# A fused attention and soft-MoE kernel on one core: routing logits in column groups, and a new order of the work inside a step

## The chip, the core and the metric

The kernel runs on one NeuronCore of a Trainium2 chip. The metric is the device time of one launch in microseconds (us); lower is better. A time is stated as the median of the runs taken, and beside it stands one profiled execution, from which every duration below is read. TensorE does matrix products and transposes, ScalarE does exponentials and copies, VectorE does copies, reciprocals and additions, GpSimd (POOL) masks and issues some loads, and the SyncE queue (SP) issues the other loads and all stores.

## The reference

The program is an attention over 8 batches of 8 heads, followed by a soft mixture of experts on the result:

```python
# q, k, v: (8, 8, 576, 64); beacon_k, beacon_v: (8, 8, 16, 64)
k_all, v_all = concat(beacon_k, k), concat(beacon_v, v)     # 592 keys per head
s = q @ k_all.T / 8;  causal mask on the 576, none on the 16 beacons
x = softmax(s) @ v_all                                      # -> (4608, 512)

logits = x @ phi                                            # (4608, 32): 8 experts x 4 slots
d = exp(logits); d /= d.sum(0)                              # over the 4608 tokens, per slot
slot_input = d.T @ x                                        # (32, 512)
slot_out[e] = relu(slot_input[e] @ w1[e]) @ w2[e]           # 512 -> 1024 -> 512
c = exp(logits); c /= c.sum(1)                              # over the 32 slots, per token
out = c @ slot_out                                          # (4608, 512)
```

So one array of exponentials, exp(x @ phi), serves twice: summed over tokens per slot, and over slots per token. (The reference subtracts maxima and adds a tiny constant to the sums, which changes nothing that matters for the time.)

## The kernel before

**Attention loop.** The loop over n runs over 32 pairs of heads; batch b is n // 4 and g is n % 4. Queries and keys are held as 16 beacon positions plus 576 tokens, 592 columns, cut in 5 chunks of 128 (the last has 80). For a pair, `transp(n, 0)` and `transp(n, 1)` turn q and k by 18 small TensorE transposes each (L265) into a PSUM tile `tr`, and VectorE copies them out (L271; ScalarE does it for a few early pairs). `score(n, st)` with st = 0 to 3 makes the transposed scores of four groups of key chunks (L282) into two PSUM tiles `sc`, used in turn: steps 0 and 2 use the first, steps 1 and 3 the second, so step 2 has to wait for the exponential of step 0, and the next pair's step 1 for that of step 3. ScalarE takes the exponential (L289), and GpSimd then zeroes the upper triangle of the diagonal blocks (L291). `attend_head(n, a)` multiplies the 15 blocks of head a with the values (L304) into one half of the PSUM tile `av`, and begins with block (0, 0), which the exponential and the mask of score step 3 make. `normalize(n)` on VectorE divides by the row sums (L314, L315) into `xb`. There is one `av`, so the next `attend_head(., 0)` follows the last `normalize`.

**Routing.** `xt_piece` turns the normalized rows (L330) into `xT`, with tokens along the free dimension. `logit_piece(b, hf)` multiplies half a batch (288 tokens) by `phih`, in which the 32 columns of phi stand four times beside each other, so that all 128 output rows carry the 32 slots four times (L344). Its exponential goes to `eLh` (L348), one long row of tokens, with the token sum taken along. `dt_piece` turns 32 rows of `eLh` back by TensorE (L356), VectorE copies the result to `dT`; `si_products` multiplies it with `xb` (L382), and `add_si` adds the product to `siacc` (L388). `col_sums` makes the sums over slots, four columns per call of a batch (L416). All PSUM tiles named `tr` share two buffers.

**The order of work** is written out by hand[...]. The first six pairs have an order of their own (`head`), and from n = 6 on each step runs the list of operations in the loop (here `s` is a score step, `T` a turn of q or k of the pair n + 2, `a` a head of the pair n - 1, `V` a turn of the values on VectorE, `C` the column sums):

```python
for op in ("s0", "s1", "Tq", "Tk", "s2", "V", "C", "a0", "dt", "s3", "lg", "xt", "lL", "si", "a1"):
    step(op, n, b, g)
```

**Loads.** q and k come on SP's queue into a ring of five pairs (L95), which `load_more` refills right after `Tk`; v comes on GpSimd's queue (L127 and neighbours), and so do the expert weights, 32 pieces of 1 MB of float32 in memory and half that on the chip (L183), at the end of a step. The last weight pieces are issued at the end of the last step.

**Tail.** After the loop come the last pair's attention, its turns, the logits of the last batch (L588, `last_logits`), the folding of `siacc` (L397), some matmuls whose result is not used (`warm_tail`, L605), the last `dt_piece`, the slot inputs (L370, L616), and the two expert layers in four passes (L642, L656), the second of which adds into `sop`. Then 9 column groups of 512 tokens are made: four matmuls of 128 tokens each (L687), copied out and scaled by ScalarE and VectorE in turn (L689, L691), and stored by SP, 1 MB per group (L695, L697).

## Time and profile before

| | |
|---|---|
| median of 5 runs | 195.86 us (195.09 to 196.31) |
| the profiled execution's own time | 195.86 us |
| its span (first to last instruction) | 193.8 us |
| TensorE busy | 157.1 us (81% of the span) |
| VectorE busy | 135.7 us (70%) |
| ScalarE busy | 129.9 us (67%) |
| GpSimd busy | 111.1 us (57%) |
| read from memory / written | 62.65 MB / 9.44 MB |
| mean granted clock of TensorE | 0.929 of full |

The profile is one execution; times in it count from the start of the span. The launch's time is 2.06 us more than its span. "Busy" is time in which an engine executes, "idle before" names what ended the wait ahead of an instruction. The matmuls' ends are modelled, and neighbouring instructions of an engine overlap a little, so the distance from one start to the next is shorter than the durations say. The DMA share is the mean busy share of the 16 DMA engines, and can exceed one where packets overlap.

### The profile page before, as it was taken

What the parts mean: (1) busy time and instruction counts of PE and PEld (TensorE: products, weight loads), DVE (VectorE), ACT (ScalarE), POOL (GpSimd) and SP (SyncE); (2) the same over time, 40 slices, a digit from 0 to 9 for tenths busy, and PEclk for the clock granted to TensorE, in tenths of its full rate; (3) what the DMA queues carried; (4) which work ended last, traced back from release to release, by engine and by line L of the source; (5) the groups of instructions that cost most, each with busy time, mean ns of one, the idle gap of its engine ahead of it and who ended that gap; (6) DMA issues with size and microseconds to landing.
All of it is one profiled execution on the core that took longest, in us unless ns stands there. A gap on an engine that the chain in (4) does not pass through costs nothing.

```text
span 193.8 us, 7205 instructions
## 1 busy us (share of the span) xinstructions
PE 157.1 (81%) x3061; PEld 108.2 (56%) x3061; DVE 135.7 (70%) x283; ACT 129.9 (67%) x190; POOL 111.1 (57%) x285
## 2 busy tenths in 40 slices
PE   6669786989887999997999797999988999787000
PEld 2437556767665777765776575577655754332000
DVE  4465587789877899996799689489845552799000
ACT  2796744789867989986788687499978222598000
POOL 8689596688776597878658567368746200000000
PEclk9975979999999999998799999699999999999955
DMA  5999999999999999999999999999999990199995
GB/s 195 266 270 350 244 283 276 264 267 271 289 260 277 297 301 270 274 252 294 267 282 283 259 308 254 238 198 205 196 213 211 215 194 14 57 405 426 411 429 225
DMA packets 20464, 50.84 MB, mean 262 GB/s; under 512 B 5456, under 2 KB 5456, under 8 KB 19408
## 3 DMA queue, kind: packets, MB, share of 16 engines
q0 software_dynamic: 8048, 21.74, 56.9%
q1 hardware_dynamic: 12240, 28.35, 39.5%
q8 instruction: 24, 0.39, 0.8%
q10 hardware_dynamic: 144, 0.29, 0.5%
q14 instruction: 8, 0.07, 0.1%
HBM read 62.65 MB, written 9.44 MB: 372 GB/s over the span
## 4 chain that ended last, share of the span: by engine, by line
PE 45%; DMA 20%; ACT 8%; DVE 7%; issue 5%; POOL 5%; SPq 1%; DVEq 0%; ACTq 0%; POOLq 0%
DMA arena<-in_k_dram 13%; PE av L304 13%; PE sc L282 10%; DMA vbuf<-in_v_dram 7%; ACT ex L289 7%; PE tr L330 4%; PE tr L265 4%; PE tr L344 3%; DVE arena L691 3%; POOL ex L291 2%; PE av L656 2%; PE sc L642 2%; DVE xb L315 2%; PE tr L382 2%; PE fp L687 1%
## 5 line engine op out<-in xcount | busy, mean ns | idle before, releaser
L289 ACT ACTIVATE ex<-sc 128x736 f16<-128x736 f32 (+1 forms) x124 | 101.5, 871 | 29.3 <-PE sc L282 26.4
L291 POOL TENSOR_SCALAR_AFFINE_SELECT ex<-ex 128x256 f16<-128x256 f16 (+1 forms) x155 | 57.8, 399 | 34.8 <-ACT ex L289 34.6
L282 PE MATMUL sc<-qT,kT 64*128 64x336 bf16 (+5 forms) x384 | 42.9, 295 | 9.0 <-ACT ex L289 4.0
L304 PEld LDWEIGHTS <-ex 128*128 128x128 f16 (+1 forms) x930 | 36.9, 108 | 11.8 <-issue 11.2
L304 PE MATMUL av<-vh,ex 128*128 128x65 f16 x840 | 39.1, 200 | 2.9 <-DVE xb L315 1.8
L265 PE MATMUL tr<-idb,arena 64*64 64x64 bf16 x1152 | 27.7, 198 | 5.0 <-DMA arena<-in_k_dram 2.9
L265 PEld LDWEIGHTS <-arena 64*64 64x64 bf16 x1152 | 23.0, 112 | 13.0 <-issue 7.0
L271 DVE COPY qT<-tr 128x576 bf16<-128x576 bf16 x32 | 23.9, 748 | 4.9 <-PE tr L265 4.7
L315 DVE TENSOR_TENSOR xb<-av,r 128x640 f16<-128x640 f32 x31 | 25.6, 824 | 1.1
L282 PEld LDWEIGHTS <-kT 64*128 64x128 bf16 (+1 forms) x384 | 16.2, 100 | 15.6 <-issue 5.8
L338 DVE COPY xT<-tr 128x592 f16<-128x592 f16 x31 | 14.0, 458 | 14.3 <-PE tr L330 14.2
L271 DVE COPY kT<-tr 128x576 bf16<-128x576 bf16 x27 | 20.3, 750 | 2.8 <-PE tr L265 2.8
L151 DVE STREAM_TRANSPOSE vh<-vbuf 128x256 f32<-128x256 f32 x32 | 20.4, 658 | 2.3 <-DMA vbuf<-in_v_dram 2.3
L183 POOL DMA_DIRECT2D arena<-in_moe_w_dram x32 | 17.9, 560 | 0.2
L127 POOL DMA_DIRECT2D vbuf<-in_v_dram x27 | 15.1, 571 | 0.2 <-issue 0.2
L330 PE MATMUL tr<-idh,xb 128*128 128x128 f16 (+1 forms) x160 | 14.4, 227 | 0.2 <-DVE xb L315 0.2
L689 ACT ACTIVATE arena<-fp,rc 128x512 f32<-128x512 f32 (+1 forms) x18 | 11.4, 676 | 4.7 <-PE fp L687 4.0
L330 PEld LDWEIGHTS <-xb 128*128 128x128 f16 (+1 forms) x160 | 10.9, 104 | 4.4 <-issue 3.4
L691 DVE TENSOR_SCALAR arena<-fp,rc 128x512 f32<-128x512 f32 (+1 forms) x19 | 12.5, 730 | 0.4 <-PE fp L687 0.4
L687 PE MATMUL fp<-soh,eLh 128*128 128x512 f16 (+1 forms) x37 | 10.8, 371 | 2.2 <-ACT arena L689 1.5
L344 PE MATMUL tr<-xT,phih 128*128 128x288 f16 x56 | 9.9, 299 | 0.2 <-DVE xT L338 0.2
L314 DVE RECIPROCAL r<-av 128x10 f32<-128x10 f32 x31 | 6.8, 220 | 4.4 <-PE av L304 3.7
(99 smaller groups left out, 134.8 us busy)
## 6 DMA issues: line engine op xcount, KB each, us to landing
arena<-in_moe_w_dram POOLq DMA_DIRECT2D x32, 512.0 KB, 9.3
arena<-in_q_dram SPq DMA_DIRECT2D x32, 288.0 KB, 15.6
arena<-in_k_dram SPq DMA_DIRECT2D x31, 288.0 KB, 15.2
out_dram<-arena SPq DMA_DIRECT2D x8, 1024.0 KB, 9.5
vbuf<-in_v_dram POOLq DMA_DIRECT2D x30, 128.0 KB, 7.7
arena<-in_v_dram POOLq DMA_DIRECT2D x4, 128.0 KB, 6.7
out_dram<-arena SPq DMA_DIRECT2D x2, 256.0 KB, 3.0
out_dram<-arena SPq DMA_DIRECT2D x1, 512.0 KB, 3.2
```

The source lines that it names most:

```text
L151: nc.vector.transpose(out=dst[:, e], in_=src.bitcast(FP).rearrange("p (j e) -> p e j", j=TK)[:, e])
L183: nc.gpsimd.dma_start(out=arena[:, wloc[m]:wloc[m] + WP], in_=src)
L265: nc.tensor.transpose(tp[po:po + 64, j, :], hi, idb[po:po + 64, po:po + 64])
L271: nc.vector.tensor_copy(out=dst, in_=src)
L282: nc.tensor.matmul(sc[0:kn, a, col:col + un], kT[n % 3][64 * a:64 * a + 64, P * c:P * c + kn], qT[n % 3][64 * a:64 * a + 64, u0:u0 + un], ...
L289: nc.scalar.activation(e, sc[:, :, 0:w], AF.Exp, scale=scale)
L291: nc.gpsimd.affine_select(out=e[0:m, :, o:o + m], in_=e[0:m, :, o:o + m], compare_op=AL.is_ge, fill=0.0, base=0, pattern=[[0, 2], [1, m]], ...
L304: nc.tensor.matmul(dst[0:m, i * DD:(i + 1) * DD], ex[n][0:kn, o + a * w:o + a * w + m], vchunk(b, 2 * g + a, c, kn), start=(c == 0), stop= ...
L315: nc.vector.tensor_tensor(out=xb[b % 2][:, :, 2 * g:2 * g + 2, :].rearrange("p i a d -> p a i d"), in0=avv[:, :, :, 0:D], in1=r5[:, :, :]. ...
L330: nc.tensor.transpose(tp[:, i, 0:m], xb[b % 2][0:m, i, 2 * g:2 * g + 2, :].rearrange("p h d -> p (h d)"), idh[0:m, 0:m])
L344: nc.tensor.matmul(lp[:, 0:w], phih[:, t, :, :].rearrange("p g s -> p (g s)"), xT[b][:, t, Nb + hf * w:Nb + (hf + 1) * w], start=(t == 0), ...
L691: nc.vector.tensor_scalar(out=osb[:, j, c], in0=fp_[:, c], scalar1=rc[:, i:i + 1], scalar2=None, op0=AL.mult)
```

## The change

The change has four parts.

1. **Column groups.** The 32 columns of phi stand in `phih` once. A batch's logits are made by 16 matmuls instead of 8: for each of the four parts of the model dimension, four matmuls whose results go to partitions 0, 32, 64 and 96, and which take every fourth block of 32 tokens, 160 columns each. The exponential of a batch is one ScalarE instruction of 128 x 160 into a compact array `eLz` at the end of `eLh`. `dt_piece` becomes one VectorE 32x32 transpose of it and a memset.
2. **Spreading.** Because the output needs the slots along 128 rows for all tokens, `spread_rows` (four matmuls with a selection matrix `rept`, and a copy of 496 columns) and `spread_ends` (three matmuls and a copy for the last 80 tokens of several batches) make `eLh` out of `eLz`. Two of these run in the tail, the others between the column groups of the output. The column sums and their reciprocals move there too, one group ahead of their use. Sums over tokens are one reduction over `eLz` and a matmul (`slot_factors`).
3. **Order in a step.** `Tq` goes between s0 and s1, the first head and `xt` go between s1 and s2, `Tk` between s2 and s3; the logits, the second head, `dt` and `si` close the step. The logits of a batch are made in the next batch's step g = 2, `dt` there too, and `si` in g = 3. In `head`, at n = 3, `turn_v(1, 1)` moves from before the attention to the end of the step.
4. **Tail.** `warm_tail` is gone; the logits of the first three parts are followed by both folds, then by the last pair's turn and the last part.

```diff
@@ -220,14 +220,19 @@
-    eLh = const.tile([P, Nb + N + P - UL], F16, name="eLh")
-    nc.vector.memset(eLh[:, Nb + N:], 0.0)
-    nc.vector.memset(eLh[:, 0:Nb], 0.0)
-    dsum9 = const.tile([P, 2 * B - 1], FP, name="dsum9")
+    ZW = NCH * 32
+    zo = N + 64 - B * ZW
+    eLh = const.tile([P, N + 64], F16, name="eLh")
+    eLz = eLh[:, zo:zo + B * ZW].rearrange("p (b i q) -> p b i q", b=B, q=32)
+    xTs = [const.tile([P, NDC * U + 48], F16, name=f"xT{i}") for i in range(2)]
+        nc.vector.memset(xTs[i][:, NDC * U:], 0.0)
+    rept = const.tile([P, 4, 4, NSL], F16, name="rept")
-    phih = const.tile([P, NDC, 4, NSL], F16, name="phih")
+    phih = const.tile([P, NDC, NSL], F16, name="phih")
...
@@ -333,34 +335,60 @@
                 idh[0:m, 0:m])
         src = tp[:, :, :].rearrange("p i u -> p (i u)")[:, 0:U]
         if act:
-            nc.scalar.activation(xT[b][:, g, :], src, AF.Copy)
+            nc.scalar.activation(xTs[b % 2][:, g * U:(g + 1) * U], src, AF.Copy)
         else:
-            nc.vector.tensor_copy(out=xT[b][:, g, :], in_=src)
-
...
+            nc.vector.tensor_copy(out=xTs[b % 2][:, g * U:(g + 1) * U], in_=src)
+
+    def logits(b, lp, ts):
+        x = xTs[b % 2][:, :]
+        for t in ts:
+            for z in range(4):
+                nc.tensor.matmul(
+                    lp[32 * z:32 * z + NSL, :], phih[:, t, :],
+                    bass.AP(tensor=x.tensor, offset=x.offset + t * U + 32 * z,
+                            ap=[x.ap[0], [P, NCH], [1, 32]]),
+                    start=(t == 0), stop=(t == NDC - 1), tile_position=(0, 32 * z))
+
+    def logit_exp(b, lp):
+        nc.scalar.activation(eLz[:, b].rearrange("p i q -> p (i q)"), lp, AF.Exp)
+
+    def logit_piece(b):
+        lp = ps_tr.tile([P, ZW], FP, name="tr", tag="tr")
+        logits(b, lp[:, :], range(NDC))
+        logit_exp(b, lp[:, :])
 
     def dt_piece(b):
         dT[b] = sml.tile([P, NCH, NSL], F16, name="dT", tag="dT", bufs=2)
-        tp = ps_tr.tile([P, NCH, NSL], F16, name="tr", tag="tr")
-        for i in range(NCH):
-            m = P if i < 4 or b == B - 1 else UL
-            nc.tensor.transpose(tp[0:m, i, :], eLh[0:NSL, b * S + P * i:b * S + P * i + m],
-                                idh[0:NSL, 0:NSL])
-        if b == B - 1:
-            nc.vector.tensor_copy(out=dT[b][:, :, :], in_=tp[:, :, :])
+        nc.vector.transpose(out=dT[b][:, :, :].rearrange("p i s -> p (i s)"),
+                            in_=eLz[:, b].rearrange("p i q -> p (i q)"))
+        nc.vector.memset(dT[b][0:Nb, 0, :], 0.0)
+
+    def spread(dst, z, src):
+        nc.tensor.matmul(dst, rept[:, z, :, :].rearrange("p t s -> p (t s)"), src,
+                         start=True, stop=True)
+
+    def evac(eng, out, in_):
+        if eng is nc.scalar:
+            nc.scalar.activation(out, in_, AF.Copy)
         else:
-            nc.vector.tensor_copy(out=dT[b][:, 0:4, :], in_=tp[:, 0:4, :])
-            nc.vector.tensor_copy(out=dT[b][0:UL, 4, :], in_=tp[0:UL, 4, :])
-        nc.vector.memset(dT[b][0:Nb, 0, :], 0.0)
+            eng.tensor_copy(out=out, in_=in_)
+
+    def spread_rows(b, eng):
+        sp = ps_tr.tile([P, 4, 4, 32], FP, name="tr", tag="tr")
+        for z in range(4):
+            spread(sp[:, :, z, :], z, eLz[:, b, 0:4, :])
+        evac(eng, eLh[:, b * S:b * S + 4 * P - Nb],
+             sp[:, :, :, :].rearrange("p i z q -> p (i z q)")[:, Nb:])
+
+    def spread_ends(b0, b1, eng, sp=None):
+        nb = b1 - b0
+        if sp is None:
+            sp = ps_tr.tile([P, nb * UL], FP, name="tr", tag="tr")[:, :]
+        spv = sp.rearrange("p (b q) -> p b q", q=UL)
+        for z in range(3):
+            w = min(32, UL - 32 * z)
+            spread(spv[:, :, 32 * z:32 * z + w], z, eLz[:, b0:b1, 4, 0:w])
+        evac(eng, eLh[:, b0 * S:b1 * S].rearrange("p (b s) -> p b s", s=S)[:, :, S - UL:], spv)
 
     def si_half(b, hf):
         sp = ps_tr.tile([P, 2, NSL], FP, name="tr", tag="tr")
...
@@ -404,17 +432,19 @@
 
     G = 4
     NG = N // (P * G)
-    csp = av[:, 0, 400:512]
+    csp = av[:, 1, 456:456 + NG * G]
     rc = const.tile([P, NG * G], FP, name="rc")
 
     def etok(cg, j):
-        o = Nb + cg * P * G
+        o = cg * P * G
         return eLh[:, o:o + P * G].rearrange("p (t j) -> p t j", j=G)[:, :, j]
 
     def col_sums(c0, c1):
+        c = slice(c0 * G, c1 * G)
         for i in range(c0 * G, c1 * G):
             nc.tensor.matmul(csp[:, i:i + 1], etok(i // G, i % G)[0:NSL], ones[0:NSL, :],
                              start=True, stop=True)
+        nc.vector.reciprocal(out=rc[:, c], in_=csp[:, c])
 
     def head(n):
         score(n, 0)
...
@@ -422,7 +452,7 @@
         score(n, 1)
         if n < 5:
             transp(m, 0)
-        for x, y in {1: ((0, 0), (0, 1)), 3: ((1, 1),), 4: ((1, 0), (1, 2))}.get(n, ()):
+        for x, y in {1: ((0, 0), (0, 1)), 4: ((1, 0), (1, 2))}.get(n, ()):
             turn_v(x, y)
         if 3 <= n < 5:
             attend_head(n - 2, 0)
@@ -461,6 +491,8 @@
                 attend_head(x, 0)
             attend_head(x, 1)
             normalize(x)
+        if n == 3:
+            turn_v(1, 1)
         if n == 4:
             turn_v(1, 3)
             transp(6, 0)
...
                     turn_v(x, y)
             if 13 <= n < 17:
                 turn_tail(1, n - 13)
-        elif op == "C" and g == 2 and b > 1:
-            col_sums(b - 2, b - 1)
         elif op[0] == "a":
             attend_head(n - 1, int(op[1]))
             if op == "a1":
                 normalize(n - 1)
         elif op == "xt":
             xt_piece(n - 2)
-        elif op == "lg" and not last and g > 1:
-            logit_piece(b - 1, g - 2)
-        elif op == "lL" and last and 0 < g < 3:
-            logit_piece(b - 1, g - 1)
-        elif op == "dt":
-            if g == 0 and b > 1:
-                dt_piece(b - 2)
-            if n == NP - 1:
-                dt_piece(b - 1)
-        elif op == "si":
-            if g == 1 and b > 1:
-                add_si(si_products(b - 2))
-            if n == NP - 1:
-                add_si(si_products(b - 1))
+        elif op == "lg" and g == 2:
+            logit_piece(b - 1)
+        elif op == "dt" and g == 2:
+            dt_piece(b - 1)
+        elif op == "si" and g == 3:
+            add_si(si_products(b - 1))
 
     for r in range(2):
         double_beacons(nc.vector, r, 0, 1)
...
@@ -526,13 +547,11 @@
         if n < 6:
             head(n)
         else:
-            for op in ("s0", "s1", "Tq", "Tk", "s2", "V", "C", "a0", "dt", "s3", "lg", "xt", "lL",
-                       "si", "a1"):
+            for op in ("s0", "Tq", "s1", "V", "a0", "xt", "s2", "Tk", "s3", "lg", "a1", "dt", "si"):
                 step(op, n, b, g)
 
         if n == 4:
-            nc.gpsimd.tensor_copy(out=phih[:, :, :, :],
-                                  in_=phif[:, :, :].unsqueeze(2).broadcast_to([P, NDC, 4, NSL]))
+            nc.gpsimd.tensor_copy(out=phih[:, :, :], in_=phif[:, :, :])
         if n == 2:
             for r in range(2):
                 double_beacons(nc.gpsimd, r, 1, B)
...
@@ -566,48 +589,31 @@
         load_w(wl)
         wl += 1
 
-    def col_sum_factors():
-        nc.vector.tensor_scalar(out=rc[:, :], in0=csp[:, 0:NG * G], scalar1=2.0 ** 8,
-                                scalar2=None, op0=AL.mult)
-        nc.vector.reciprocal(out=rc[:, :], in_=rc[:, :])
-
     L = B - 1
 
     avl = scs[0]
     for rows in ((4,), (3, 2, 1), (0,)):
+        if rows == (0,):
+            spread_rows(0, nc.vector)
         for a in range(2):
             attend_blocks(NP - 1, a, avl[:, a, :], [(c, i) for i in rows for c in range(i + 1)])
     normalize(NP - 1, avl)
     xt_piece(NP - 2, True)
-    lps = [scs[1][:, hf, 0:S // 2] for hf in range(2)]
-
-    def last_logits(ts):
-        for hf in range(2):
-            for t in ts:
-                o = Nb + hf * (S // 2)
-                nc.tensor.matmul(lps[hf], phih[:, t, :, :].rearrange("p g s -> p (g s)"),
-                                 xT[L][:, t, o:o + S // 2],
-                                 start=(t == 0), stop=(t == NDC - 1))
-
-    last_logits([0, 1])
+    lp = scs[1][:, 0, 0:ZW]
+    logits(L, lp, [0, 1, 2])
     fold_si(0)
+    fold_si(1)
     xt_piece(NP - 1)
-    last_logits([2])
-    fold_si(1)
-    last_logits([3])
-    for hf in range(2):
-        o = Nb + L * S + hf * (S // 2)
-        nc.scalar.activation(eLh[:, o:o + S // 2], lps[hf], AF.Exp)
-    col_sums(6, 7)
-
-    def warm_tail(k):
-        for _ in range(k):
-            nc.tensor.matmul(scs[0][:, 1, :], idh[:, :], xT[L][:, 0, 0:512],
-                             start=True, stop=True)
-
-    warm_tail(3)
+    logits(L, lp, [3])
+    logit_exp(L, lp)
+    spread_rows(1, nc.scalar)
     dt_piece(L)
-    warm_tail(2)
+    nc.gpsimd.memset(eLz[64:96, :, 4, UL - 64:32], 0.0)
+    nc.gpsimd.memset(eLz[96:P, :, 4, :], 0.0)
+    nc.gpsimd.memset(eLz[0:32, :, 0, 0:Nb], 0.0)
+    foldr = qT[2][:, 0:2 * P].bitcast(FP).rearrange("p (t s) -> p t s", s=NSL)
+    nc.gpsimd.tensor_copy(out=foldr, in_=fold[:, :].unsqueeze(1).broadcast_to([P, 4, NSL]))
+    spread_ends(0, 4, nc.scalar, av[:, 1, 128:128 + 4 * UL])
     ds = siz[:, :, :, :]
     for hf in range(2):
         sp = si_half(L, hf)
...
@@ -620,14 +626,17 @@
                 in1=siT[:, c, :].rearrange("p (e s) -> p e s", e=E),
                 op0=AL.mult, op1=AL.add)
 
-    dsum = const.tile([P, 1], FP, name="dsum")
+    nc.vector.reduce_sum(out=dsz[:, :], in_=eLz.rearrange("p b i q -> p (b i q)"),
+                         axis=mybir.AxisListType.X)
     rd = const.tile([P, 1], FP, name="rd")
-    nc.vector.reduce_sum(out=dsum9[:, 2 * L:2 * L + 1], in_=eLh[:, Nb + L * S:Nb + N],
-                         axis=mybir.AxisListType.X)
-    nc.vector.reduce_sum(out=dsum[:, :], in_=dsum9[:, :], axis=mybir.AxisListType.X)
-    nc.vector.tensor_scalar(out=dsum[:, :], in0=dsum[:, :], scalar1=2.0 ** -16, scalar2=None,
-                            op0=AL.mult)
-    nc.vector.reciprocal(out=rd[:, :], in_=dsum[:, :])
+
+    def slot_factors():
+        ps = av[:, 1, 504:505]
+        nc.tensor.matmul(ps, foldr.rearrange("p t s -> p (t s)"), dsz[:, :],
+                         start=True, stop=True)
+        nc.vector.tensor_scalar(out=rd[:, :], in0=ps, scalar1=2.0 ** -8, scalar2=None,
+                                op0=AL.mult)
+        nc.vector.reciprocal(out=rd[:, :], in_=rd[:, :])
 
     sop = av[:, 0, :]
     hbuf = exq.tile([P, 2, 2, 4, P], F16, name="hbuf", tag="ex")
...
@@ -663,8 +672,8 @@
         if p < EP:
             first_layer(p)
         if p == 1:
-            col_sums(7, NG)
-            col_sum_factors()
+            col_sums(0, 1)
+            slot_factors()
         if 0 < p <= EP:
             turn_hidden(p - 1)
         if p > 1:
@@ -695,6 +704,14 @@
                 nc.sync.dma_start(out=dst[:, w, :], in_=osb[:, w, :])
         if cg > 0:
             nc.sync.dma_start(out=dst, in_=osb[:, :, :])
+        if cg + 2 < B:
+            spread_rows(cg + 2, (nc.scalar, nc.vector)[cg % 2])
+        if cg == 1:
+            spread_ends(4, B - 1, nc.scalar)
+        if cg == 5:
+            spread_ends(B - 1, B, nc.scalar)
+        if cg + 1 < NG:
+            col_sums(cg + 1, cg + 2)
 
 
 # ---- launch: one core; inputs and outputs as the reference has them ----
```

## The prediction

> **What bounds the kernel now.** I read the page first, then stretches of the run one by one, then single steps in order of time. The stretches:
>
> ```profile
> core 0: us, PE busy (x) PEld busy (x) DVE busy (x) ACT busy (x) POOL busy (x), PEclk, DMA share, GB/s
> 128.00:148.00 20.00, 18.02 (x373) 13.19 (x371) 13.98 (x28) 17.45 (x29) 14.02 (x37) 1.00 1.06 207
> 160.00:162.30 2.30, 2.30 (x43) 1.12 (x40) 0.42 (x1) 0.61 (x2) 0.00 (x0) 1.00 0.12 23
> 162.30:167.50 5.20, 4.49 (x61) 2.03 (x59) 2.21 (x6) 1.19 (x3) 0.00 (x0) 1.00 0.00 0
> 180.00:191.00 11.00, 0.00 (x0) 0.00 (x0) 0.00 (x0) 0.00 (x0) 0.00 (x0) 0.65 1.00 419
> ```
>
> There are three stages. Until 160 us the DMA engines are full (share 1.06) with loads; until 167.5 only the tail's compute runs; then stores run at 419 GB/s until the end, and the engines are done by 180. So the stores cost what 9.44 MB cost, and the end follows the first store. That follows the tail, the tail follows the end of attention, and the last weights, which land by 162.3, are a second floor. They are needed by the last quarter of the second layer, at about 165.2 (163.74 + 3/4 of 1.91), so compute can win at most about 3 us before it waits for them.
>
> One step of the loop, in order of time (start, duration, engine):
>
> ```profile
> 133.25 0.41 POOL L291 TENSOR_SCALAR_AFFINE_SELECT ex<-ex 128x256 f16<-128x256 f16 x1 [0.55 <-ACT ex L289]
> 133.40 0.48 PE L282 MATMUL sc<-qT,kT 64*128 64x208 bf16 x8
> 133.81 0.76 PE L265 MATMUL tr<-idb,arena 64*64 64x64 bf16 x36
> 133.83 2.24 ACT L289 ACTIVATE ex<-sc 128x736 f16<-128x736 f32 x3 [0.26 <-PE sc L282]
> 134.67 0.37 PE L282 MATMUL sc<-qT,kT 64*128 64x464 bf16 x2
> 134.97 0.63 PE L304 MATMUL av<-vh,ex 128*128 128x65 f16 x14
> 135.57 0.30 PE L356 MATMUL tr<-idh,eLh 32*128 32x32 f16 x5
> 135.80 0.39 PE L282 MATMUL sc<-qT,kT 64*128 64x512 bf16 x2
> 136.12 0.44 PE L330 MATMUL tr<-idh,xb 128*128 128x128 f16 x5
> 136.40 0.62 PE L304 MATMUL av<-vh,ex 128*128 128x65 f16 x14
> 136.99 0.64 PE L282 MATMUL sc<-qT,kT 64*128 64x208 bf16 x8
> ```
>
> TensorE hardly stops. From start to start: s0 and s1 0.41, turns with the wait for the first exponential 0.86, s2 0.30, a head 0.60, dt 0.23, s3 0.32, xt 0.28, a head 0.59: 3.59 us, 3.36 without dt. Read in the same way, half a batch of logits is 0.57, si 0.50, column sums 0.21. A batch of four steps is 4 x 3.36 + 2 x 0.57 + 0.23 + 0.50 + 0.21, or 15.5 us. TensorE bounds this stage, and every gap in it counts in full.
>
> Earlier, the loads set the pace. In the chain that ended last:
>
> ```profile
> 41.76 19.14 DMA arena<-in_k_dram
> 60.94 0.47 PE tr L265 x18
> ```
>
> A k that took 19 us stops the turns until 60.94. And two gaps of over 1.3 us (at 88 and 120, "issue" in the waits) each cost a slow stretch afterwards, as this shows:
>
> ```profile
> 87.60:91.00 3.40, 2.25 (x61) 1.70 (x59) 2.31 (x4) 2.30 (x3) 3.40 (x10) 1.00 1.08 321
> 91.00:94.40 3.40, 3.40 (x38) 2.48 (x38) 1.62 (x4) 1.77 (x5) 2.08 (x6) 0.51 1.04 253
> ```
>
> A window in which TensorE is busy 66% is followed by one at half clock.
>
> [...]
>
> **The change part by part.** Relative to the span of 193.8 us; the execution took 195.86, which is also the median, so 2.06 lies around the span.
>
> *Logits.* A batch loses 8 matmuls (1.14) and gains 16 small ones. At 28 ns each, as the 20 small ones of L370 show (0.57 us), that is 0.45. ScalarE loses two exponentials of 0.41 and two reads of 0.20 and gains one of 128 x 160, about 0.30 by the slope of the rows 288 (405 ns) and 1024 (1025 ns). Turning back costs TensorE nothing now (0.23 saved); [...] Column sums leave (0.21). TensorE's own work per batch falls from 15.5 to 4 x 3.22 + 0.45 + 0.50 = 13.8.
>
> *The new order* adds a wait. The first head of pair n - 1 now follows s1 directly; it opens with block (0, 0), whose exponential is the last of the pair before, and mask. From the end T of that exponential: mask starts at +0.07 (133.18 to 133.25), ends +0.48, head from +0.54 to +1.14, xt to +1.42, s2; its exponential starts 0.43 after it (as s0 at 133.40 and 133.83 show), at +1.85. Then 0.88 to the next exponential's start and 1.02 for it: 3.75. This ring is the new step. Behind the waiting head in TensorE's queue stand xt and s2, and ScalarE waits for s2. Before, the head came after s2 and the same ring had 2.6, hidden. TensorE has some 0.5 of slack in it for logits and si, but the second head's end moves by 0.45 in a logits step and `normalize` holds `av` against the next head: +0.4; `add_si` on VectorE +0.27 a step later. A batch takes 4 x 3.75 + 0.67 = 15.7 against 15.5: +0.9 over the 4.75 batches from step 12. So 1.7 us less TensorE work a batch gains nothing there by itself.
>
> It gains elsewhere. The late k stops TensorE after the first head, xt and s2 rather than before them: -1.2 (0.60 + 0.28 + 0.31), once. k's load is issued later in the step, behind the later `Tk` on SP's queue; with the DMA engines full its landing is not set by that, but up to +1 if it were. The three gaps over 1.2 us (88, 107, 120) fall into a stage with slack: -0.4 each, -1.2. The last three steps took 12.35 us (137.42 to 149.77), with waits for exponentials; on the ring 3.84 + 2 x 3.75 + 0.05, -0.9. `turn_v(1, 1)` no longer stops VectorE at 21 to 23 us, which the loads of the next 40 us swallow. Sum at the end of attention: -2.4, my range -4.5 to +2.
>
> *Tail.* These lines hold the old one:
>
> ```profile
> 151.86 0.66 ACT L336 ACTIVATE xT<-tr 128x592 f16<-128x592 f16 x1 [2.09 <-PE tr L330]
> 153.95 0.71 ACT L600 ACTIVATE eLh<-sc 128x288 f16<-128x288 f32 x2 [1.43 <-PE sc L588]
> 154.16 0.82 PE L605 MATMUL sc<-xT,idh 128*128 128x512 f16 x3
> 155.66 0.67 PE L370 MATMUL tr<-dT,xb 128*128 128x32 f16 x20
> 163.74 1.91 PE L656 MATMUL av<-arena,hbuf 128*32 128x512 f16 x32
> ```
>
> From the last exponential's end (149.77) to L370 is 5.89. New, from the same point: normalize of the last pair ends at +2.83 (+2.61 before), since `add_si` and a spread's copy stand ahead of it on VectorE; but the logits wait for ScalarE's copy until +2.2 and both folds (1.0) follow them, so the turn starts at +3.4, its copy ends +4.35, the exponential +5.05 (0.30 instead of 0.71), the VectorE transpose and memset +5.5. GpSimd's first two memsets of `eLz` wait for the transpose, and `spread_ends` on TensorE waits for them: +5.95, and 0.2 for its matmuls. The slot inputs start at +6.15: +0.3. `warm_tail` also kept TensorE busy (4.90 of 5.10 us between 151.3 and 156.4). Without it I count 2.9 of the 4.8 us up to +6.15 (logits 0.6, folds 1.1, turn 0.4, spreads 0.8), 60%, less than the 66% above; a half clock under the first layer costs up to 1.7 us. Windows of 3.4 us fall as they fall: half of that, +0.8.
>
> *Output.* Per group ScalarE or VectorE gets a copy of 496 columns (0.6) and VectorE a reciprocal (0.2): about 2.0 us per group instead of 1.36, while 1 MB takes 2.5 us to store. Hidden, from the second group on; without that cover, up to 7 x 0.6. The first store waits for nothing new. 0, bounds 0 and +0.7.
>
> Sum: -2.4 + 0.3 + 0.8 + 0 is -1.3; a span of 192.5 and a time of 194.6.
>
> **Rivals.** *Full gain*: the clock stays up and TensorE's slack takes more of the gaps. The floor of the weights stops it at -3: 192.9 or a little less. For it: TensorE bounds the loop. Against: the ring.
> *No change*: gaps come at other places, the clock falls fully: -2.4 + 0.3 + 1.7, within 0.6 of before.
> *Slower by the mask ring*: it stands on one masking step, one PSUM pass and two semaphores. 20 steps from step 12 lie on it, so a ring of 3.82 instead of 3.75 eats the forecast's gain, and from there each 0.1 costs 2 us; at 3.95 the end comes at 198.6. For it: GpSimd waits for ScalarE and ScalarE for TensorE in the longest rows of the waits; GpSimd also issues loads between masks (0.55 each). Against: the terms are all read from the trace.
> The change does what it says in any case: its instructions stand in the new order.
>
> **How the numbers follow.** A measurement here tells about 0.3%, 0.6 us. Forecast case (195.2 to 193.4) 0.32, full gain 0.22: faster 0.54. No change 0.14. Slower by the ring or the tail 0.32. The range leaves out the deepest gain and the worst of the slow case: 192.4 to 198.2; the forecast case alone, 193.4 to 195.2.
>
> **What would show it.** Right: step starts 3.7 to 3.9 apart, TensorE waiting for GpSimd ahead of L309 once a step, ScalarE idle some 0.6 ahead of the third exponential; the last exponential ends near 147.4; spread matmuls waiting for GpSimd memsets before the slot inputs; stores without gaps. Wrong: steps of 4 us or more, half-clock stretches in the first layer, a wait of the last second-layer matmuls for weights, or stores that starve.

## The result, and the profile after

The changed kernel takes 197.9 us (median of 41 runs, 195.31 to 202.02) against 195.94 us of the kernel before on the same chips (78 runs): a ratio of 1.008, 95% interval 1.0057 to 1.0103. It is slower by 2.0 us by the medians (1.6 us by the ratio), where 1.3 us less had been forecast. The ratios here leave disturbed executions out, so they can lie a little beside the quotient of two medians. The profiled execution is one of the longer ones (200.04 us, span 198.3), so that its single places are read here against other executions too.

The stretches of the changed kernel that answer to those of before (columns: stretch, its length, busy time and instructions of each engine, granted clock, DMA share, GB/s):

```profile
core 0: us, PE busy (x) PEld busy (x) DVE busy (x) ACT busy (x) POOL busy (x), PEclk, DMA share, GB/s
128.00:148.00 20.00, 17.01 (x382) 11.88 (x380) 14.64 (x29) 15.55 (x21) 13.68 (x37) 1.00 1.06 215
158.40:161.90 3.50, 3.06 (x33) 1.12 (x25) 1.40 (x2) 1.20 (x2) 0.00 (x0) 0.51 0.92 185
161.90:168.70 6.80, 6.80 (x114) 3.24 (x114) 1.92 (x6) 1.19 (x2) 0.00 (x0) 1.00 0.08 16
184.00:195.00 11.00, 1.44 (x9) 0.63 (x8) 2.65 (x5) 2.26 (x4) 0.00 (x0) 0.73 1.01 419
```

The three stages are there as before. In the loop TensorE is busy for 17.0 of 20 us instead of 18.0; how much of that is less work and how much is more waiting is counted further down. The stores run at 419 GB/s as before. New is the second stretch: the granted clock was 0.51 just where the first expert layer runs.

Put one after the other, the profiled execution of before and that of after differ so (us; the span is longer by 4.45):

| from the span's start or the point above | before | after | difference |
|---|---|---|---|
| end of the last exponential of attention | 149.77 | 151.12 | +1.35 |
| to the first matmul of the first layer | 6.67 | 6.86 | +0.19 |
| to the start of the last matmul of the second layer | 8.83 | 10.71 | +1.88 |
| to the first store | 2.30 | 2.30 | 0 |
| to the landing of the last store | 25.21 | 25.95 | +0.74 |
| to the end of the span | 1.03 | 1.33 | +0.30 |

One step of the loop in the changed kernel, TensorE's rows (start, duration), which come in the order of the list of operations, and then VectorE's `normalize` in it:

```profile
131.04 0.34 PE L287 MATMUL sc<-qT,kT 64*128 64x208 bf16 x6
131.31 0.47 PE L270 MATMUL tr<-idb,arena 64*64 64x64 bf16 x18
131.71 0.32 PE L287 MATMUL sc<-qT,kT 64*128 64x336 bf16 x2
132.28 0.61 PE L309 MATMUL av<-vh,ex 128*128 128x65 f16 x14 [0.25 <-DVE xb L320]
132.73 0.20 PE L309 MATMUL av<-vt,ex 80*80 80x65 f16 x1
132.77 0.43 PE L332 MATMUL tr<-idh,xb 128*128 128x128 f16 x5
133.13 0.37 PE L287 MATMUL sc<-qT,kT 64*128 64x464 bf16 x2
133.43 0.47 PE L270 MATMUL tr<-idb,arena 64*64 64x64 bf16 x18
133.83 0.39 PE L287 MATMUL sc<-qT,kT 64*128 64x512 bf16 x2
134.15 0.63 PE L309 MATMUL av<-vh,ex 128*128 128x65 f16 x14
```

```profile
131.40 0.82 DVE L320 TENSOR_TENSOR xb<-av,r 128x640 f16<-128x640 f32 x1
```

The first head (132.28) does wait, but for VectorE: `normalize` of the pair before has to be done with the one `av` (131.40 + 0.82 = 132.22) before the head may write to it. That is the commonest wait of TensorE in this kernel. The mask is close behind it, though: of twelve heads between 60 and 150 us that were held by `normalize` for 0.1 us or more, five had their mask done only 0.06 to 0.07 us earlier than `normalize`. TensorE's waits from 40 to 150 us (total, number, longest):

```profile
PE av L309 <- DVE xb L320: 4.1, 13, 0.7
PE tr L270 <- DMA arena<-in_q_dram: 3.8, 5, 1.3
PE tr L270 <- DMA arena<-in_k_dram: 1.8, 3, 1.4
```

The same of the kernel before:

```profile
PE sc L282 <- ACT ex L289: 3.0, 3, 1.4
PE tr L265 <- DMA arena<-in_k_dram: 2.6, 3, 1.3
```

The waits for exponentials fell to one of 0.5 us, and waits for `normalize` and for q came: q is now turned ahead of the second score step. The late load that the prediction saw in the chain is no single event either; in this execution eight turns waited for a q or a k, 5.6 us together, against three and 2.6 us for a k before.

The tail, in order of time:

```profile
154.40 0.42 PE L332 MATMUL tr<-idh,xb 128*128 128x128 f16 x5
...
156.02 0.35 DVE L362 STREAM_TRANSPOSE dT<-eLh 128x160 f16<-128x160 f16 x1 [0.69 <-ACT eLh L353]
...
157.08 0.30 PE L367 MATMUL av<-eLh,rept 128*128 128x128 f16 x3 [1.11 <-POOL eLh L612]
...
157.22 0.66 PE L398 MATMUL tr<-dT,xb 128*128 128x32 f16 x20
...
157.98 3.20 PE L651 MATMUL sc<-arena,siz 128*32 128x512 f16 x32
```

The slot inputs (L398) start 6.10 us after the last exponential; 6.15 had been worked out. Ahead of them TensorE waits for GpSimd's memsets, as forecast. The last row holds the first two passes of the first layer: 3.20 us. In the kernel before they took 1.91:

```profile
156.44 1.91 PE L642 MATMUL sc<-arena,siz 128*32 128x512 f16 x32
```

The windows just ahead of the first layer and under it, in the changed kernel:

```profile
155.00:158.40 3.40, 1.79 (x39) 1.38 (x42) 1.41 (x8) 1.32 (x3) 0.94 (x4) 1.00 1.06 213
158.40:161.90 3.50, 3.06 (x33) 1.12 (x25) 1.40 (x2) 1.20 (x2) 0.00 (x0) 0.51 0.92 185
```

and in the kernel before, with `warm_tail`:

```profile
153.00:156.40 3.40, 3.28 (x42) 1.95 (x40) 1.27 (x6) 0.71 (x2) 0.00 (x0) 1.00 1.06 212
156.40:159.80 3.40, 3.36 (x60) 1.74 (x60) 2.28 (x10) 1.19 (x2) 0.00 (x0) 1.00 0.96 193
```

TensorE was busy for 53% of the one and 96% of the other; half clock followed the first.

### The profile page after: what moved, and what is told of

Same layout as the page of the kernel before. It is cut to its first block, busy times and chain, and to the rows that moved or that the text cites. A ratio compares the mean times of both kernels' runs of the same rounds, so it can differ in the third digit from the quotient of the medians.

```text
span 198.3 us, 7324 instructions
## 1 busy us (share of the span) xinstructions
PE 156.6 (79%) x3123; PEld 106.5 (54%) x3123; DVE 139.5 (70%) x286; ACT 127.5 (64%) x175; POOL 113.2 (57%) x293
## 5 line engine op out<-in xcount | busy, mean ns | idle before, releaser
L287 PE MATMUL sc<-qT,kT 64*128 64x336 bf16 (+5 forms) x384 | 46.4, 298 | 3.3 <-ACT ex L294 1.9
L309 PEld LDWEIGHTS <-ex 128*128 128x128 f16 (+1 forms) x930 | 37.5, 108 | 19.7 <-issue 13.2
L270 PE MATMUL tr<-idb,arena 64*64 64x64 bf16 x1152 | 31.6, 200 | 9.2 <-DMA arena<-in_q_dram 3.8
L270 PEld LDWEIGHTS <-arena 64*64 64x64 bf16 x1152 | 24.7, 113 | 20.1 <-issue 7.1
L151 DVE STREAM_TRANSPOSE vh<-vbuf 128x256 f32<-128x256 f32 x32 | 20.4, 656 | 0.2 <-DMA arena<-in_v_dram 0.2
L340 DVE COPY xT<-tr 128x592 f16<-128x592 f16 x31 | 13.4, 436 | 5.1 <-PE tr L332 5.1
L332 PE MATMUL tr<-idh,xb 128*128 128x128 f16 (+1 forms) x160 | 14.2, 221 | 0.5 <-issue 0.5
L700 DVE TENSOR_SCALAR arena<-fp,rc 128x512 f32<-128x512 f32 (+1 forms) x19 | 13.1, 732 | 1.2 <-PE fp L696 0.4
L332 PEld LDWEIGHTS <-xb 128*128 128x128 f16 (+1 forms) x160 | 10.4, 103 | 0.8 <-issue 0.6
L696 PEld LDWEIGHTS <-eLh 128*128 128x128 f16 x37 | 3.9, 113 | 5.7 <-issue 4.6
```

The lines of the kernel that those rows point to most:

```text
L151: nc.vector.transpose(out=dst[:, e], in_=src.bitcast(FP).rearrange("p (j e) -> p e j", j=TK)[:, e])
L270: nc.tensor.transpose(tp[po:po + 64, j, :], hi, idb[po:po + 64, po:po + 64])
L287: nc.tensor.matmul(sc[0:kn, a, col:col + un], kT[n % 3][64 * a:64 * a + 64, P * c:P * c + kn], qT[n % 3][64 * a:64 * a + 64, u0:u0 + un], ...
L309: nc.tensor.matmul(dst[0:m, i * DD:(i + 1) * DD], ex[n][0:kn, o + a * w:o + a * w + m], vchunk(b, 2 * g + a, c, kn), start=(c == 0), stop= ...
L332: nc.tensor.transpose(tp[:, i, 0:m], xb[b % 2][0:m, i, 2 * g:2 * g + 2, :].rearrange("p h d -> p (h d)"), idh[0:m, 0:m])
L696: nc.tensor.matmul(fp_[:, c], etok(cg, j), soh[:, c], start=True, stop=True)
```

## The experiments

**Theories.** A: the unused matmuls that went with `warm_tail` held the clock, and it now falls under the first layer. B: the order in the step costs or gains. C: the output starts up later. D: the loads pace the loop. E and F, formed later: VectorE, or its `normalize` on the one `av`, has taken TensorE's place.

### The clock in the tail

*e1_warm*, the changed kernel with five unused matmuls put back:

```diff
     spread_rows(1, nc.scalar)
+    warm_tail(3)
     dt_piece(L)
+    warm_tail(2)
```

> The changed kernel with the five unused matmuls of 512 columns put back into its tail: three ahead of the last batch's turning back, two behind it, so that they fill the wait ahead of spread_ends. Theory A (the clock in the tail): in the profile of the changed kernel TensorE ran at half clock from 158.4 to 161.9 and the first two passes of the first layer took 3.20 us against 1.91; with the filler that stretch goes away, the two passes take 1.9 to 2.0, and the time falls by 1 to 1.9 us, to a ratio of about 1.000. Theory B (the order in the step loses the time before the tail): no change, a ratio of 1.007 to 1.011. Theory C (the output's start loses it): no change either.

195.85 us, ratio 1.0003 (0.9966 to 1.004). The loss is no longer there. Its own profile, of a longer execution (198.70 us), still has a half-clock stretch (155.6 to 159.1), after a window with 69% busy, and from the last exponential to the last matmul of the second layer it takes 17.40 us there, hardly less than the 17.57 (6.86 + 10.71) of the changed kernel. So it is the total of e1 that speaks for the clock, and not its trace; e7 has such a trace.

*e6_before_no_warm*, the kernel before with both calls of `warm_tail` left out.

> The kernel before without its five unused matmuls in the tail, and nothing else. Theory A (they hold the clock, and their loss is the whole loss of the change): half clock under the first layer in most executions, 1.6 us, ratio 1.007 to 1.009. If the old tail is busy enough without them (logits of 592 columns in 8 matmuls, turned on TensorE): the five matmuls lie in a wait for the exponential anyway, ratio 0.998 to 1.002, and the clock under the first layer is a matter of the new tail's waits.

197.07 us against 195.96, ratio 1.0018 (0.9974 to 1.0062): a loss that the interval does not settle, and less than the 1.007 to 1.009 that theory A had expected here. Its profile shows the same in the old tail:

```profile
153.30:156.70 3.40, 2.50 (x45) 1.74 (x48) 1.52 (x9) 0.71 (x2) 0.00 (x0) 1.00 1.06 213
156.70:160.20 3.50, 3.50 (x44) 1.51 (x36) 1.40 (x6) 1.20 (x2) 0.00 (x0) 0.51 1.04 208
```

74% busy, then half clock. The first layer starts 0.25 us sooner (6.42 us after the last exponential instead of 6.67), and the expert layers take 10.24 us instead of 8.83, together 1.2 us more in this execution.

*e7_more_warm*, the changed kernel with 11 unused matmuls:

```diff
     logits(L, lp, [0, 1, 2])
+    warm_tail(3)
...
     xt_piece(NP - 1)
+    warm_tail(3)
...
     spread_rows(1, nc.scalar)
+    warm_tail(3)
     dt_piece(L)
+    warm_tail(2)
```

> The changed kernel with 11 unused matmuls of 512 columns in the three waits of its tail (3 in the wait for ScalarE's copy of x^T, 3 in the wait for VectorE's copy, 5 around the turn of the weights). Theory A: the first layer is at full clock in its profile; it gains what the five alone still left (a half-clock stretch from 155.6 in the profile of that run, about 1 us), ratio 0.993 to 0.998 against before. If the clock was already up in most executions with five: the same ratio as with five, 0.997 to 1.003. If unused matmuls push the tail's own work back: 1.004 or more.

195.88 us, ratio 1.0009 (0.9978 to 1.004): as with five. The clock is full under the first layer (94% busy ahead of it), but the matmuls stand in TensorE's queue ahead of the tail's own work: 7.47 us from the last exponential to the first layer instead of 6.86. Together that is 16.88 us instead of 17.57, against 15.50 before. And at full clock the expert layers still take 9.41 us instead of 8.83. Here is why, in the second pass of this kernel:

```profile
155.35 1.48 DVE L639 TENSOR_REDUCE dsz<-eLh 128x1 f32<-128x1280 f16 x1
...
157.43 0.18 DVE L447 RECIPROCAL rc<-av 128x4 f32<-128x4 f32 x1 [0.61 <-PE av L445]
...
157.76 0.35 PE L645 MATMUL av<-dsz,qT 128*128 128x1 f32 x2 [0.44 <-DVE rc L447]
```

`slot_factors` is a matmul in TensorE's queue, ahead of the turn of the hidden layer. It waits for VectorE, which has a reduction of 1.48 us and the reciprocal ahead of it. In the changed kernel the same row stands at 161.84, also with 0.44 of waiting.

All profiled executions of the study, taken together, speak for A. Seven are of kernels without unused matmuls in the tail (after, e2, e4, e12, e14 and e16 with the changed tail, e6 with the old one): the clock fell under the first layer in all seven. Thirteen are of kernels with them: it fell in one, e1.

How busy a window has to be is less clear. In the traces the granted clock changes in steps of 3.41 us: in the changed kernel it was half for one such step from 158.4, in the kernel before for one from 91.0 and one from 121.8. Of 791 such windows at full clock in the 20 profiles (from 5 us to 35 us ahead of the end), 20 had TensorE busy for less than 55%, and half clock followed each of them; 649 had it busy for 75% or more, and half clock followed none. Between the two it went either way: half clock followed 37 windows, full clock 85, as here in the changed kernel:

```profile
69.70:73.10 3.40, 2.03 (x58) 1.47 (x58) 2.15 (x5) 1.72 (x3) 3.36 (x8) 1.00 1.03 274
73.10:76.50 3.40, 2.58 (x73) 1.94 (x66) 2.48 (x5) 2.14 (x3) 1.75 (x4) 1.00 1.08 275
```

So the window of 66% on which the prediction built was the rarer case: of 44 windows between 65 and 70%, full clock followed 36. What decides between 55 and 75% is open.

### The order of the step

*e2_old_order*, the changed kernel with the order `s0 s1 Tq Tk s2 V a0 s3 lg xt a1 dt si`.

> The changed kernel (column groups, spreading, new tail) with the old order in a step from n = 6 on: s0 s1 Tq Tk s2 V a0 s3 lg xt a1 dt si. Theory B: the last attention exponential ended 1.35 us later in the changed kernel's profile, because Tq ahead of s1 stops everything behind it when q is late, and the first head waits for the mask; with the old order and 1.7 us less TensorE work a batch attention ends 1 to 3 us earlier than with the new order, ratio 0.993 to 1.003. Theory A: the tail is the same, so the ratio stays near 1.008 to 1.010, whatever the loop does. The ring of my prediction (3.75 us a step) would make the two orders equal.

197.84 us, ratio 1.0111 (1.0076 to 1.0145): no better than the changed kernel. In its profile (197.12 us) attention ends at 148.15, 3.0 us sooner than in the longer one of the changed kernel, but the first layer starts 7.68 us later than that instead of 6.86: the tail takes a part of what the loop gives.

*e3_before_new_order* was meant to do the converse, but put the slot inputs behind the second head, so that rows of a later batch were in their sums: a part of the computation changed, and with it the waits (208.05 us, ratio 1.0637). It tells nothing on the order.

> The kernel before with only the order in a step changed from n = 6 on: s0 Tq s1 V a0 xt s2 Tk s3 lg lL a1 C dt si; logits, spreading, tail and output are as before. Theory B: slower, ratio 1.005 to 1.012, with more TensorE waits for q and for GpSimd, and the last attention exponential later by 1 to 2 us. Theory A and C: within 0.3% of before, since the tail and the output are the old ones.

*e5_before_new_order* mends that (`s0 Tq s1 V a0 xt s2 Tk s3 lg lL C dt si a1` in the kernel before).

> The kernel before with the turns, the first head and x^T in the places of the new order (slot inputs and column sums still of the batch before the last, ahead of the second head, so that all of the computation stays). Order is harmless (as the run that took the order back out of the changed kernel says): ratio 0.996 to 1.004. The ring over the mask, as the slow case of the prediction had it: the end of attention 2 us later or more, ratio 1.01 or more. The gain that the prediction gave to the order (late k, gaps, last steps: 3.3 us less 0.9): ratio 0.988.

196.39 us, ratio 1.0037 (1.001 to 1.0064). By itself the order costs 0.2 to 1.2 us, and surely does not gain the 2.4 us that were expected of it. The waits of its heads for `normalize` are the longest (6.6 us, 23 times, from 40 to 150 us; 4.1 us and 13 times in the changed kernel).

### Parts of the tail and the output

*e4_ends_later*, the changed kernel with `spread_ends(0, 4, ...)` behind the slot inputs.

> The changed kernel with the call of spread_ends for batches 0 to 3 moved behind the slot inputs' matmuls, so that these no longer wait for the GpSimd memsets. In the changed kernel's profile that wait was 1.33 us, of which the slot inputs could have used 0.6 to 0.7. All theories: the slot inputs start 0.6 to 0.7 us earlier, and the time falls by as much, ratio about 1.005, or by more if the shorter idle stretch keeps the clock up (theory A).

199.55 us in 6 runs, no interval. In its profile the slot inputs start only 0.1 us sooner (6.01 us after the last exponential): the wait for GpSimd hid nearly nothing behind it, since they then wait for the transpose and its memset (0.58 us).

*e8_warm_output*, e7 with the column sums of the output one group earlier and the spread of batch 2 in the expert layers:

```diff
-        if cg + 1 < NG:
-            col_sums(cg + 1, cg + 2)
+        if cg + 2 < NG:
+            col_sums(cg + 2, cg + 3)
```

> As the run with 11 unused matmuls, and besides the column sums and reciprocals one group earlier (group 1 in the second pass of the expert layers) and the spreading of batch 2 ahead of the output loop. Theory C (the ramp of the output is late by the added work of groups 0 and 1): from the first store to the last landing 25.2 as before instead of 25.6 to 25.95, 0.4 to 0.7 us less than the run with 11 unused matmuls, ratio 0.002 to 0.004 lower than it. If the stores are paced by the DMA engines anyway: no difference, or the expert layers 0.3 us longer.

199.21 us, ratio 1.0195 (1.0134 to 1.0256). Earlier sums made the output slower: 28.4 us from the first store to the last landing. TensorE's waits in the first groups (168 to 182 us) say why:

```profile
PE av L445 <- DVE eLh L374: 2.2, 2, 1.2
PE av L445 <- ACT eLh L372: 0.7, 1, 0.7
```

The sums of group `cg + 2` need the spread that is issued just ahead of them. Its copy stands behind the group's own copies on VectorE or ScalarE, and behind the waiting sums stand the next group's matmuls. Full groups are issued 3.2 to 3.6 us apart, where 1 MB takes 2.4 to 2.5 us to land in the changed kernel.

*e9_new_tail* lays the tail out anew:

```diff
-    logits(L, lp, [0, 1, 2])
+    logits(L, lp, [0, 1])
+    warm_tail(2)
+    logits(L, lp, [2])
     fold_si(0)
-    fold_si(1)
     xt_piece(NP - 1)
+    fold_si(1)
...
     spread_rows(1, nc.scalar)
+    warm_tail(2)
     dt_piece(L)
...
-            slot_factors()
+        if p == 3:
+            slot_factors()
```

and has `spread_ends(0, 4, ...)` behind the slot inputs.

> The changed kernel with its tail laid out anew: the turn of the last pair's rows stands between the two halves of the fold instead of behind both (0.6 us sooner by the profile of the changed kernel, where VectorE is done at 153.81 and the turn starts at 154.40), the spread of the batch ends stands behind the slot inputs (0.1), the slot factors two passes later in the expert layers (their wait for the 1.48 us reduction stopped TensorE for 0.5 to 0.6 us in the second pass), and four unused matmuls stand in the two waits. Tail theory (A, with the parts of the tail that the prediction did not count): from the end of the last exponential to the last matmul of the second layer 15.5 to 16.2 us instead of 17.6, ratio 0.990 to 0.996. If the loop has lost what the tail loses, that is, if the loss does not lie in the tail: 1.002 or more.

195.65 us, ratio 0.9982 (0.995 to 1.0014). From the last exponential to the last matmul of the second layer it takes 15.39 us (6.38 + 9.01) instead of 17.57, a little less than before (15.50). The clock is full. With `slot_factors` two passes later the expert layers take 9.01 us, not 9.41 as in e7. The total is that of before all the same; the 0.990 to 0.996 that had been expected did not come.

*e10_new_tail_output*, the same with the spreads and the sums both one group earlier, so that no sum waits for its own spread.

> As the run with the new tail, and the spreads and the column sums of the output each one group earlier (so that no column sum waits for the spread issued just ahead of it, which made 3.3 us of each group in the run with only the sums moved). Theory C: from the first store to the last landing 25.2 us or less, ratio 0.001 to 0.004 below the run with the new tail. If the stores alone pace the output: the same ratio. If the two more spreads hold up the expert layers: 0.002 above.

195.22 us, ratio 0.9979 (0.9951 to 1.0006): no difference to e9. From the first store to the last landing 25.37 us. Theory C falls: nine profiled executions with the changed output have 25.35 on the mean (24.93 to 25.95), seven with the old one 25.33 (24.70 to 26.00). The 0.74 of the first comparison was that one execution.

### What bounds the loop

*e11_before_less_w* and *e12_after_less_w* leave out half of the weight loads.

```diff
+    for m in range(NPC):
+        if m // 4 % 2:
+            wloc[m] = wloc[m - 4]
     def load_w(i):
         m = worder[i]
+        if m // 4 % 2:
+            return
```

> The kernel before without the weight loads of experts 1, 3, 5 and 7, which use the weights of experts 0, 2, 4 and 6 instead: a part of the computation changed, 8.4 of 41.4 MB of loads gone, no instruction of the engines other than the loads. TensorE theory (as the prediction had it, 15.5 us a batch): the steps from 12 to 30 keep their 4.33 us less only the waits for loads, the end of attention at 145 to 150. Load theory (D: the loop takes as long as its loads take, at 260 GB/s, whatever TensorE has to do): the end of attention 10 to 25 us sooner, steps of 3.6 to 4.0 us.

> The changed kernel with the same loads left out (experts 1, 3, 5 and 7 use the weights of the expert ahead of them: a part of the computation changed). Load theory (D): with fewer loads the work on TensorE counts, and now the 1.7 us a batch less show: the end of attention 4 to 9 us sooner than in the kernel before with the same loads, steps of 3.3 to 3.75 us. Ring over the mask (the prediction's): no sooner than there, steps of 3.75 to 3.9. TensorE theory without loads: as with all loads, 0 to 2 us.

189.44 us (ratio 0.9634, 0.9549 to 0.9719) and 191.13 us (0.9772, 0.9702 to 0.9842). Both win: against their own kernels 0.037 and 0.031 in the ratio, or 7.2 and 6.0 us, each with an interval of some 1.5 us to either side. The steps from 12 to 30 fall from 4.33 to 4.06 and from 4.42 to 3.92. Attention ends at 146.50 in e11, 3.3 us sooner than before, where theory D had 10 to 25. From 120 to 140 us, e11 and then e12:

```profile
120.00:140.00 20.00, 18.70 (x409) 13.55 (x405) 16.53 (x33) 17.04 (x26) 10.41 (x31) 1.00 0.71 139
```

```profile
120.00:140.00 20.00, 18.30 (x416) 13.01 (x415) 15.12 (x31) 16.86 (x23) 12.05 (x34) 1.00 0.57 95
```

With the DMA engines at 71 and 57% the loop is faster, and four of the 18 steps take 3.59 us in e11 and 3.40 or 3.41 in e12; but with all loads the shortest are the same (three of 3.59 before, two of 3.41 after). In these two profiles the changed kernel is ahead, by 2.5 us in the 18 steps and by 5.1 us at the end of attention (141.38). But the one of e11 lies 3.1 us above its median and the one of e12 1.5 us below, and by the ratios e12 is the slower one, by 2.7 us, of which the tail is 2.1. So no gain of the changed loop shows with fewer loads either. Loads are a part of what bounds the loop and not the whole. That GpSimd issues 16 loads less (0.56 us each, between masks) came with it and was not told apart.

*e13_before_pe* and *e14_after_pe* add work to TensorE, *e15_before_dve* and *e16_after_dve* to VectorE, in each step from pair 12 or 13 on:

```diff
+                if op == "s3" and n >= 12:
+                    for _ in range(8):
+                        nc.tensor.matmul(av[:, 1, 328:448], idh[:, :], idh[:, 0:120],
+                                         start=True, stop=True)
```

```diff
+                if op == "a1" and n > 12:
+                    nc.vector.memset(siz[:, :, :, :], 0.0)
```

> The kernel before with 8 unused matmuls of 120 columns behind the fourth score step of each step from pair 12 on (20 x 8; at the 50 to 60 ns of the attention matmuls 0.4 to 0.5 us a step, 8 to 10 us in all). TensorE bounds the loop (the prediction's first step): each costs in full, steps of 4.75 to 4.85 instead of 4.33, 8 us or more, ratio 1.04 or more. Another bound: much of it is swallowed by waits, 0 to 4 us, ratio 1.00 to 1.02.

> The changed kernel with the same 8 unused matmuls a step. If what the change took off TensorE has turned into waits for VectorE and loads (theory E): 0 to 4 us over the changed kernel, less than they cost in the kernel before, ratio 1.01 to 1.03 against before. If TensorE bounds this one too: 8 us or more over the changed kernel, ratio 1.05 or more.

> The kernel before with one memset of 1024 columns on VectorE behind each normalize from pair 13 on (zeros over zeros; [...]19 of them). TensorE bounds the loop: swallowed, ratio 0.998 to 1.005. VectorE is a bound here as well (88% busy with this loop): two thirds or more of 19 times its duration, ratio 1.02 or more.

> The changed kernel with the same memset behind each normalize. Theory E (VectorE's normalize holds the one av bank against the next first head, the waits before the first head that the trace puts down to it): it costs two thirds or more of 19 times its duration over the changed kernel, more than in the kernel before. Loads pace the loop instead: swallowed, 1.006 to 1.012 as the changed kernel without it.

The added matmuls start 54 to 57 ns apart on the mean, so 160 of them are 8.6 to 9.1 us. They cost 7.9 us in the kernel before (204.28 against 196.35; ratio 1.0417, 1.0225 to 1.0608). In the changed one the ratio is 1.0412 (1.0283 to 1.0542), 0.033 or 6.5 us over the 1.008 that it has without them. VectorE's addition, in e16:

```profile
L553 DVE MEMSET siz<- 128x512 uint32 x19 | 9.2, 485 | 1.1
```

9.2 us of it cost nothing in the kernel before (195.19 us, ratio 1.001, 0.997 to 1.005). In the changed one the ratio is 1.0146, with an interval from 0.9997 to 1.0296 that holds the 1.008 without it; two thirds of 9.2 us, as theory E had it, would be a ratio of 1.039. In its profile the steps from 12 to 30 take 4.29 us. So theory E falls: VectorE has room. Time added to TensorE behind the fourth score step counts for the most part, in both kernels: some 90% before, some 75% after. The intervals of 0.013 to 0.019 on these ratios are 2.5 to 3.7 us, so that half is not excluded.

*e17b_new_tail_old_order* and *e18b_second_head_early*, on top of e10, take the wait for `normalize` away: by the old order, and by `s0 Tq s1 V a0 s2 Tk a1 s3 lg xt dt si`.

> The run with the new tail and the earlier output, with the old order of the step. Theory F (in the new order the first head waits for VectorE's normalize of the pair before, which frees the one `av` bank, as in 13 to 23 of the steps of every kernel with the new order; the old order has five operations between the second head and the next first one and never waits there): ratio 0.988 to 0.994, below the run with the new order by 0.003 to 0.008, no wait of the heads for VectorE. If the order tells nothing (as the changed kernel with the old order says): 0.995 to 1.001, as with the new order.

> The run with the new tail and the earlier output, with the new order changed in one thing: the second head stands ahead of the fourth score step, and x^T behind the logits, so that normalize has the fourth score step, the logits, x^T and the next pair's first three operations to hide behind. Theory F: the waits of the heads for VectorE go, ratio 0.988 to 0.994. If ScalarE then waits for the fourth score step instead (0.6 us later): 1.00 or more.

195.09 us, ratio 0.9982 (0.995 to 1.0014), and 196.09 us, ratio 0.9978 (0.9941 to 1.0016), against 0.9979 of e10. The wait went in both, and the time stayed; 0.988 to 0.994 had been expected. In e18b the heads wait for the mask instead, which was close behind `normalize` before:

```profile
PE av L309 <- POOL ex L296: 3.5, 12, 1.7
```

Theory F falls as a cause of the total.

What became of TensorE's time can be counted, from each matmul's start to the next one's, over the 18 steps from pair 12 to 30. Two neighbours have a usual distance at which nothing waits: 0.32 us from a score step of 512 columns to a turn of rows behind it, 0.30 from one of 464 columns to a head, 0.13 to 0.14 from a turn or a head to the score step behind it. (It was taken from all profiles, as the tenth percentile for each pair of neighbours, and as the upper quartile inside a block of equal matmuls.) The sum of the usual distances is TensorE's own time. What a distance has beyond the usual one, when over 0.02 us, is a wait:

| us over 18 steps | before | e5 (new order, old logits) | e2 (old order, columns) | after | e11 | e12 |
|---|---|---|---|---|---|---|
| own time | 65.4 | 67.9 | 61.4 | 64.1 | 64.8 | 63.6 |
| all waits | 12.5 | 9.2 | 14.6 | 15.5 | 8.3 | 6.9 |
| of these ahead of heads | 1.9 | 5.5 | 4.4 | 7.0 | 0.9 | 5.4 |
| ahead of turns of q and k | 2.2 | 0.9 | 6.5 | 5.9 | 1.7 | 0.8 |
| 18 steps | 77.9 | 77.1 | 75.9 | 79.6 | 73.1 | 70.6 |

The column groups did take work off: 4.0 us of own time, from before to e2. But the new order puts most of it back: 2.7 us from e2 to after, 2.5 from before to e5, 2.5 from e17b (61.6) to e10 (64.1). In the old order TensorE passes between a score step and other work six times in a step, in the new order eight times, and each passage costs 0.13 to 0.32 us from start to start even when nothing waits (in the step shown above, 133.13 to 133.43 and 133.83 to 134.15). So TensorE's own time is only 1.3 us less after the whole change, in 18 steps, and 3.0 us more of waits stand in this execution, ahead of heads and turns.

## Why the prediction was wrong, point by point

- **The end of attention, -2.4, did not come; this is the step that failed.** Over seven profiled executions with the changed loop as it is (after, e1, e4, e7, e8, e9, e10) the last exponential ends at 147.72 to 151.76, on the mean 150.15; with the loop of before at 149.77 and 149.72. That is +0.4. Five of the seven lie 1.1 to 2.9 us above the median of their kernel, and the two that lie below it (e7, e10) end attention at 147.72 and 147.95, near the forecast 147.4, so that this mean is somewhat too high. By difference, an estimate: of the total of +1.6 (ratio) or +2.0 us (medians) the tail below is +2.1, which leaves -0.5 to -0.1 for the loop.
- **Which of its terms failed.** The late k (-1.2): pair 12 starts at 61.67 to 65.53 in the seven, 63.21 on the mean, against 63.92 and 63.62, so at most half of it, within the spread. The last three steps (-0.9): from the start of pair 29 to the last exponential's end 11.96 to 12.24 us in six of the seven (17.8 in e4) against 12.78, so -0.5 to -0.8. Between the two, from pair 12 to 29, the ring (+0.9) and the gaps (-1.2) were to make -0.3; it is +0.8 (73.98 on the mean against 73.06 and 73.31). The gaps did not fall into slack. Starts on TensorE that lie more than 1.2 us apart were three in these pairs of the kernel before and two in e6, and are one to three in each of the seven, at other places.
- **The slack that was to take them in was hardly there.** TensorE's own time was to fall from 15.5 to 13.8 us a batch. Of these 1.7, 0.56 (3.36 to 3.22 in each step) had no instruction behind it (at most it is the wait that was read with the turns), and the new order was priced at nothing in TensorE's queue. Counted over the 18 steps, 4.5 batches, it falls from 14.5 to 14.2 us a batch: the columns save 0.9, the order costs 0.6 of it. "TensorE hardly stops" was read from one step of 3.59 us; three of the 18 are that short, the mean is 4.33, and 12.5 of 77.9 us are waits. That adding to TensorE costs most of its price (e13, e14) says that it is on the path; the change just took little away from it, and waits at other places grew.
- **The ring over the mask, +0.9 in the middle steps, was near in its sum by luck.** The 18 steps are 0.6 us longer on the mean of the seven (4.36 us a step against 4.33), but a step of 3.75 was forecast, with the ring behind it, and the steps that differ from this are longer by waits for other things or, twice, shorter (3.41). The head waits for GpSimd's mask only once by the waits shown by the profile (0.2 us), where it was to do so in each step; it waits for `normalize` 13 times, with the mask 0.06 to 0.07 us ahead of it in five of the waits counted above. Of the other signs, ScalarE's 0.66 us ahead of the third exponential came (0.6 forecast), and so did both the steps of over 4 us and the half clock in the first layer, which were named as signs of being wrong.
- **The tail, +0.3, was right**: +6.10 against +6.15, by the steps named, and +6.09 in e12. The price in it of the 16-bit VectorE transpose was the author's estimate, which no run had shown: with the memset behind it, 0.45 us were taken from the end of the exponential (+5.05 to +5.5), and it was 0.51 (155.98 to 156.49, the transpose itself 0.35). Missed behind it was the place of `slot_factors`: 0.6 us of expert layers at full clock (9.41 against 8.83), a wait for VectorE in TensorE's queue, of which e9 takes 0.4 away by placing it later. The prediction priced the reduction nowhere.
- **The clock, +0.8, was right in kind, at half its size.** A busy share of 60% was counted, and "windows fall as they fall" then halved the cost. The last window came out at 53%, the clock fell in all six profiled executions with the changed tail and no unused matmuls, and it costs 1.3 us (10.71 against 9.41; 3.20 against 1.91 in the first two passes).
- **The output, 0, was right**: 25.35 against 25.33 us.
- **The rivals**: "no change" had the clock in full and was nearest in that. "Slower by the mask ring" gave the sign but the wrong place: the steps are hardly longer (4.36 against 4.33), the tail is.

With the measured terms the tail's sum is +0.2 + 0.6 + 1.3 + 0, or +2.1 us, against +2.0 by the medians and +1.6 by the ratio. The loss lies in the tail: e9 takes it away with a new layout, and its trace shows the tail at 15.39 us against 15.50 before; the total of e1, with five unused matmuls, agrees. That the loop gave less than 2.4 us is in part accounted for by the passages in TensorE's queue. Why waits of 9 to 16 us stay in 18 steps with all loads is open: single causes (VectorE's time, `normalize`, the order) were taken away one at a time and another wait took their place; GpSimd's masks and load issues, and ScalarE, were not varied by themselves.

## What to carry to other kernels

Before work is taken off an engine, add up its own time from start to start in the new order, and not only the instructions that go: here a new order with two more passages in a step took back two thirds of what fewer matmuls saved. Count waits over many steps and not in one. Where unused matmuls stand in waits ahead of a dense stretch, count the busy share of the window of 3.4 us ahead of it without them: here half clock followed all 20 windows under 55%, 37 of the 122 from 55 to 75%, and none of the 649 above. A matmul whose operand comes from another engine's long operation belongs as late in TensorE's queue as its use allows (`slot_factors` two passes later; the column sums a group behind their spread).
